# Retention followed by a leaky-ReLU MLP on one core: the order of ScalarE and VectorE work behind TensorE's products, and the engine that applies the masks

## The chip, the cores and the metric

One core of a Trainium2 chip. The metric is the device time of one execution in microseconds (us). Kernels sent together ran on the same chip, in alternation with the kernel before.

## The reference

Two stages. Retention: for 8 batches and 8 heads, scores of q and k are multiplied by a decay that depends on the distance and applied to v. Then an MLP over the 4608 resulting tokens.

```python
scores = scale * np.matmul(q, k.transpose(0, 1, 3, 2))       # q, k, v: (8, 8, 576, 64)
ret = scores * Dmat[None]                                    # gamma ** (i - j), i >= j
x = np.matmul(ret, v)                                        # -> 4608 tokens x 512
h = x @ w_in                                                 # 512 x 2048
g = np.maximum(0.01 * h, h)
return g @ w_out                                             # 2048 x 512
```

## The kernel before

Retention is done in 36 units of 128 tokens, as linear attention with a running state; four units make a set of 512 tokens for the MLP. From set 2 on, both layers save matmuls by Strassen-like schemes: seven products in place of eight, with sums of operands made beforehand (`sum_x` on GpSimd, `mix` on VectorE) and sums of products made while the PSUM banks are read (`plus`, `keep`, `give`). While a set goes through the MLP, four "bursts" of the next units' retention are put between its products: two in the first layer (`at_step(5)`, `at_step(6)`), two in the second (`at_step(7)`, `at_step(8)`). The first layer's group of seven:

```python
    def h_seven(g, f, fill, middle=None):
        ...

        def plus(name, a, b):
            r[name] = m_pool.tile([P, 2, HT], FP, name=name)
            nc.vector.tensor_tensor(out=r[name], in0=r[a], in1=r[b], op=ADD)

        def give(i, k, name):
            leaky(g_tile(g)[:, f + i * HF : f + i * HF + 2, k * HT : (k + 1) * HT], r[name])

        product("p1", w_sub(f, 0, 0), x_sub(g, 0, 0), True)
        r["k1"] = m_pool.tile([P, 2, HT], FP, name="k1")
        nc.scalar.copy(out=r["k1"], in_=r["p1"])
        fill[0]()
        product("p1", w_sub(f, 0, 1), x_sub(g, 1, 0), False)
        give(0, 0, "p1")
        fill[1]()
        product("p6", w[:, 1], t[:, 1], True)
        plus("u2", "p6", "k1")
        product("p5", w[:, 0], t[:, 0], True)
        plus("v", "p5", "u2")
        if middle is not None:
            middle()
        fill[2]()
        product("p7", w[:, 2], t[:, 2], True)
        plus("h4", "p7", "v")
        product("p5", w[:, 3], x_sub(g, 1, 1), False)
        plus("h5", "p5", "u2")
        give(1, 1, "h4")
        fill[3]()
        give(0, 1, "h5")
        product("p7", w_sub(f, 1, 1), t[:, 3], False)
        plus("h4", "p7", "u2")
        give(1, 0, "h4")
```

`middle` is the burst. `fill` are ordinary blocks of the first layer that give the other engines time. p1, p5 and p7 are accumulated into twice; a second pass must wait until the first result has been read out of its bank: k1 is such a reading (by ScalarE), h4 and `v` are others (by VectorE).

The burst, the masks and the loop over the sets:

```python
    def masks(u, aside=False):
        s16s[u] = b_pool.tile([P, 2, NP, CH], F16, name="s16")
        if aside:
            nc.scalar.copy(out=s16s[u], in_=sc_tiles[u][:, :, 0])
            nc.gpsimd.tensor_tensor(
                out=s16s[u],
                in0=s16s[u],
                in1=mask16.unsqueeze(1).unsqueeze(1).to_broadcast([P, 2, NP, CH]),
                op=MUL,
            )
            return
        nc.vector.tensor_tensor(
            out=s16s[u],
            in0=sc_tiles[u][:, :, 0],
            in1=mask_sb.unsqueeze(1).unsqueeze(1).to_broadcast([P, 2, NP, CH]),
            op=MUL,
        )

    def burst(u, out=True):

        if u < NU:
            scores(u)
        if out:
            outputs(u - 1)
        if u < NU:
            masks(u, u > 12)
            state(u, 0)
            state(u, 1)
            state_cast(u, pool_copy)
        if out:
            own(u - 1)
            add(u - 1)
        ...

        def at_step(n):
            return (lambda: step(4 * g + n)) if more else None

        h_seven(g, 0, [block(2), block(10), block(3), block(11)], at_step(5))
        mix(g, 0, 0)
        mix(g, 1, 0)
        h_seven(g, 4, [block(6), block(7), block(14), first], at_step(6))
        mix(g, 2, 0)
        h_block(g, 15)
        for n in range(3):
            mix(g, n, 1)
        others({0: [at_step(7)], 4: [at_step(8)]} if more else {})
```

For units after the twelfth, ScalarE copies the scores out of PSUM and GpSimd, which gets its operands from SBUF here, multiplies by the mask. `state` adds to the running state on VectorE; at every fourth chunk it needs a further multiplication by the decay, with both operands in SBUF (line 275; it is called the "scaled addition" below, though it is a multiplication).

## Time and profile before

| | before |
|---|---|
| time, median of 3 runs first, of 6 with those beside the change | 294.28, 294.17 us |
| profiled span | 292.0 us |
| TensorE / VectorE / ScalarE / GpSimd busy | 276.3 / 211.7 / 158.3 / 160.7 us |
| length of a set (sets 2 to 7, from one first copy of p1 to the next) | 29.5 to 30.6 us |
| holes over 0.1 us in TensorE's stream in sets 2 to 8, by cause: K, H, M, X | 6.25, 2.26, 1.36, 0.43 us |

A hole is read from the starts of two matmuls; the wait that the timeline prints in brackets is smaller, as it counts from the modelled end of the last matmul. K is the wait for the copy k1, H the one for the addition h4, M the one for the mixing addition, X the one for GpSimd's input sums.

### The profile page before, as it was taken

Reading aid. Unit: us, or ns where it says so; the run is one execution under the profiler, and the core shown is the slowest. Engines: PE = TensorE matmul, PEld = TensorE weight load, DVE = VectorE, ACT = ScalarE, POOL = GpSimd, SP = SyncE. Lnnn points to the kernel's source line nnn. Section 1 sums busy time; section 2 is a strip of 40 time slices with the busy share of each in tenths; the row PEclk is TensorE's granted clock in tenths of the full one; section 3 lists DMA queues with packets and bytes.
Section 4 is the critical chain, followed back from the end, with each engine's and each line's share of the span. In section 5 each row is a group of like instructions: output and inputs, shape, how many; then the busy total and the mean of one; then the engine's idle time right before and its main releaser. Section 6 shows DMA issues by size and latency. Waiting matters only on the chain.

```text
span 292.0 us, 9901 instructions
## 1 busy us (share of the span) xinstructions
PE 276.3 (95%) x4279; PEld 205.0 (70%) x4279; DVE 211.7 (73%) x352; ACT 158.3 (54%) x292; POOL 160.7 (55%) x175
## 2 busy tenths in 40 slices
PE   7799999999999999899979998999899998999994
PEld 2478889547876787578747875687578856785774
DVE  2983787987857795779586968886779577866572
ACT  4676767425247824782477357644765376517520
POOL 8968503563385649554964489438943892151000
PEclk9999999999999999999999999999999999999999
DMA  8999999999999979973999589668976341011003
GB/s 218 295 234 226 275 205 222 188 200 195 243 232 295 225 149 243 219 167 87 181 250 175 122 186 257 142 140 169 270 145 147 71 147 38 2 74 72 2 0 144
DMA packets 131739, 50.03 MB, mean 171 GB/s; under 512 B 121264, under 2 KB 126000, under 8 KB 131696
## 3 DMA queue, kind: packets, MB, share of 16 engines
q1 hardware_dynamic: 125392, 39.59, 60.2%
q0 software_dynamic: 6016, 9.70, 14.9%
q8 instruction: 33, 0.54, 0.8%
q10 hardware_dynamic: 288, 0.11, 0.2%
q14 instruction: 10, 0.08, 0.1%
HBM read 36.81 MB, written 9.44 MB: 158 GB/s over the span
## 4 chain that ended last, share of the span: by engine, by line
PE 69%; DVE 16%; ACT 8%; DMA 2%; issue 2%; POOL 2%; DVEq 0%; ACTq 0%; POOLq 0%
PE acc L588 27%; PE acc L390 19%; PE acc L470 12%; ACT gt L404 6%; PE acc L525 5%; DVE mix L569 5%; DVE h L481 3%; PE sc L220 2%; DMA t<-in_q_dram 2%; DVE s L271 1%; DVE xT L377 1%; DVE s L275 1%; ACT k L488 1%; DVE v L481 1%; PE sc L229 1%
## 5 line engine op out<-in xcount | busy, mean ns | idle before, releaser
L390 PE MATMUL acc<-xT,w_in 128*128 128x512 f16 (+2 forms) x544 | 88.7, 304 | 0.3 <-DVE xT L377 0.2
L404 ACT ACTIVATE gt<-acc 128x512 f16<-128x512 f32 x102 | 60.0, 597 | 17.9 <-PE acc L390 16.3
L588 PEld LDWEIGHTS <-gt 128*128 128x128 f16 x640 | 61.2, 98 | 8.5 <-ACT gt L404 0.8
L390 PEld LDWEIGHTS <-w_in 128*128 128x128 f16 x544 | 46.3, 98 | 17.4 <-issue 0.3
L240 POOL TENSOR_TENSOR s<-s,idle 128x512 f16<-128x512 f16 x23 | 27.3, 1186 | 41.9 <-ACT s L239 41.9
L588 PE MATMUL acc<-w_out,gt 128*128 128x256 f16 x384 | 46.3, 273 | 0.2 <-ACT gt L404 0.2
L177 POOL TENSOR_TENSOR qk<-t,cs 128x512 f16<-128x512 f32 x28 | 30.3, 1082 | 19.8 <-DMA t<-in_q_dram 19.8
L239 ACT CAST s<-sc 128x512 f16<-128x512 f32 x23 | 13.4, 584 | 36.1 <-PE sc L229 36.1
L404 ACT ACTIVATE gt<-h 128x512 f16<-128x512 f32 x42 | 25.9, 628 | 12.4 <-DVE h L481 11.8
L181 POOL TENSOR_TENSOR v<-t,cs 128x512 f16<-128x512 f32 x28 | 30.1, 1076 | 1.7 <-DMA t<-in_v_dram 1.4
L588 PE MATMUL acc<-w_mix,mix 128*128 128x256 f16 x256 | 30.3, 273 | 0.4
L588 PE MATMUL acc<-w_mix,gt 128*128 128x256 f16 x256 | 30.6, 273 | 0.0
L481 DVE TENSOR_TENSOR u<-acc,k 128x512 f32<-128x512 f32 x14 | 9.7, 691 | 26.6 <-PE acc L470 26.6
L470 PEld LDWEIGHTS <-w_sum 128*128 128x128 f16 x224 | 21.9, 98 | 9.1 <-issue 0.5
L174 ACT CAST qk<-t 128x512 f16<-128x512 f32 x36 | 22.6, 627 | 10.5 <-DMA t<-in_k_dram 10.5
L588 PEld LDWEIGHTS <-mix 128*128 128x128 f16 x256 | 24.5, 98 | 4.9 <-DVE mix L569 2.0
L470 PEld LDWEIGHTS <-w_in 128*128 128x128 f16 x168 | 15.9, 97 | 15.6 <-issue 7.1
L372 ACT COPY own<-ot 128x512 f32<-128x512 f32 x33 | 19.5, 591 | 12.6 <-PE ot L316 7.1
L287 POOL CAST st<-s 128x512 f16<-128x512 f32 x21 | 13.0, 621 | 23.9 <-DVE s L275 10.2
L377 DVE TENSOR_TENSOR xT<-ot,own 128x512 f16<-128x512 f32 x33 | 22.5, 682 | 4.9 <-ACT own L372 4.9
L481 DVE TENSOR_TENSOR h<-acc,u 128x512 f32<-128x512 f32 x28 | 19.2, 685 | 8.4 <-PE acc L470 8.4
L470 PE MATMUL acc<-x_sum,w_sum 128*128 128x256 f16 x168 | 22.9, 272 | 0.3 <-POOL x_sum L457 0.3
(77 smaller groups left out, 424.8 us busy)
## 6 DMA issues: line engine op xcount, KB each, us to landing
out_dram<-osb SPq DMA_DIRECT2D x17, 512.0 KB, 4.3
t<-in_k_dram SPq DMA_DIRECT2D x27, 256.0 KB, 3.6
t<-in_q_dram SPq DMA_DIRECT2D x26, 256.0 KB, 4.0
t<-in_v_dram SPq DMA_DIRECT2D x25, 256.0 KB, 4.5
w_in<-in_moe_w_in_dram POOLq DMA_DIRECT2D x8, 256.0 KB, 6.7
w_out<-in_moe_w_out_dram POOLq DMA_DIRECT2D x4, 512.0 KB, 10.0
t<-in_v_dram POOLq DMA_DIRECT2D x7, 256.0 KB, 5.3
t<-in_q_dram POOLq DMA_DIRECT2D x6, 256.0 KB, 5.6
```

The lines of the kernel that those rows point to most:

```text
L174: nc.scalar.copy(out=qk16[u][:, 1], in_=t32[u, 1])
L177: eng.tensor_tensor(out=qk16[u][:, 0], in0=t32[u, 0], in1=decay(u, 0), op=MUL)
L181: eng.tensor_tensor(out=v16[u], in0=t32[u, 2], in1=decay(u, 1), op=MUL)
L240: nc.gpsimd.tensor_tensor(out=s16s[u], in0=s16s[u], in1=mask16.unsqueeze(1).unsqueeze(1).to_broadcast([P, 2, NP, CH]), op=MUL,)
L372: nc.scalar.copy(out=owns[u], in_=ot_tiles[u][:, :, 0:NP].rearrange("q j c t -> q c j t"))
L377: nc.vector.tensor_tensor(out=x_of(u).rearrange("q (c g) t -> q c g t", g=2), in0=ot_tiles[u][:, :, NP : 2 * NP].rearrange("q g (c j) t -> ...
L390: nc.tensor.matmul(out=hps[:, n, :], lhsT=w_in16[:, c, f * P : (f + 1) * P], rhs=xT[g][:, c, ts], start=(c == 0), stop=(c == NP - 1),)
L404: nc.scalar.activation(out=out, in_=in_, func=mybir.ActivationFunctionType.Lrelu)
L470: nc.tensor.matmul(out=r[name][:, n, :], lhsT=lhs[:, c, n * P : (n + 1) * P], rhs=rhs[:, c, :], start=fresh and n == 0 and c == 0, stop=c ...
L481: nc.vector.tensor_tensor(out=r[name], in0=r[a], in1=r[b], op=ADD)
L525: nc.tensor.matmul(out=ys[tb], lhsT=g_t[0][:, f, tb * P : (tb + 1) * P], rhs=w_out16[:, f, :], start=(f == 0), stop=(f == NF - 1),)
L588: nc.tensor.matmul(out=r[name][tb][:, 0, :] if apart else r[name][0][:, tb, :], lhsT=lhs[:, f, tb * P : (tb + 1) * P], rhs=rhs[:, f, :], s ...
```

## The change

The intent: (1) the last two activations of one group of seven go behind the next group's copy k1, so that this copy isn't held up, and the first two mixing additions (`mix`) go with them; (2) in the first layer's bursts, the output sum of the retention goes behind the two additions h4 and h5, which free banks of PSUM; (3) the masks of the two bursts in the second layer go from ScalarE and GpSimd to VectorE.

```diff
--- before.py
+++ after.py
@@ -456,7 +456,7 @@
         ):
             nc.gpsimd.tensor_tensor(out=t[:, n], in0=a, in1=b, op=SUB)
 
-    def h_seven(g, f, fill, middle=None):
+    def h_seven(g, f, fill, middle=None, owed=()):
 
         r = {}
         t = x_sums[g]
@@ -486,6 +486,8 @@
         product("p1", w_sub(f, 0, 0), x_sub(g, 0, 0), True)
         r["k1"] = m_pool.tile([P, 2, HT], FP, name="k1")
         nc.scalar.copy(out=r["k1"], in_=r["p1"])
+        for late in owed:
+            late()
         fill[0]()
         product("p1", w_sub(f, 0, 1), x_sub(g, 1, 0), False)
         give(0, 0, "p1")
@@ -494,19 +496,19 @@
         plus("u2", "p6", "k1")
         product("p5", w[:, 0], t[:, 0], True)
         plus("v", "p5", "u2")
-        if middle is not None:
-            middle()
+        settled = middle() if middle is not None else None
         fill[2]()
         product("p7", w[:, 2], t[:, 2], True)
         plus("h4", "p7", "v")
         product("p5", w[:, 3], x_sub(g, 1, 1), False)
         plus("h5", "p5", "u2")
+        if settled is not None:
+            settled()
         give(1, 1, "h4")
         fill[3]()
-        give(0, 1, "h5")
         product("p7", w_sub(f, 1, 1), t[:, 3], False)
         plus("h4", "p7", "u2")
-        give(1, 0, "h4")
+        return [lambda: give(0, 1, "h5"), lambda: give(1, 0, "h4")]
 
 
 
@@ -780,19 +782,21 @@
             mix(g, n, 0)
             mix(g, n, 1)
 
-    def burst(u, out=True):
+    def burst(u, out=True, split=False):
 
         if u < NU:
             scores(u)
         if out:
             outputs(u - 1)
         if u < NU:
-            masks(u, u > 12)
+            masks(u, split)
             state(u, 0)
             state(u, 1)
             state_cast(u, pool_copy)
         if out:
             own(u - 1)
+            if split:
+                return lambda: add(u - 1)
             add(u - 1)
 
     def ahead(u, between=None):
@@ -810,10 +814,11 @@
         if u < NU:
             load(u)
 
-    def step(u):
-        burst(u)
+    def step(u, split=False):
+        rest = burst(u, True, split)
         fetch(u + 4)
         ahead(u + 2, (lambda: sum_x(u // 4 - 1)) if u % 4 == 0 else None)
+        return rest
 
 
     halves(0, (0, 1))
@@ -934,13 +939,17 @@
         def block(f):
             return lambda: h_block(g, f)
 
-        def at_step(n):
-            return (lambda: step(4 * g + n)) if more else None
-
-        h_seven(g, 0, [block(2), block(10), block(3), block(11)], at_step(5))
-        mix(g, 0, 0)
-        mix(g, 1, 0)
-        h_seven(g, 4, [block(6), block(7), block(14), first], at_step(6))
+        def at_step(n, split=False):
+            return (lambda: step(4 * g + n, split)) if more else None
+
+        owed = h_seven(
+            g, 0, [block(2), block(10), block(3), block(11)], at_step(5, True)
+        )
+        owed += [lambda: mix(g, 0, 0), lambda: mix(g, 1, 0)]
+        for late in h_seven(
+            g, 4, [block(6), block(7), block(14), first], at_step(6, True), owed
+        ):
+            late()
         mix(g, 2, 0)
         h_block(g, 15)
         for n in range(3):
```

## The prediction

> **What bounds the kernel now.** I read the page first (shares, clock, chain), then the waits of one set, then the timeline of that set. A "set" is 512 tokens; sets 2 to 8 run the loop that the change edits, sets 0 and 1 and the start do not. The page says that TensorE is the bound, at full clock:
>
> ```profile
> span 292.0 us, 9901 instructions
> ...
> PE 276.3 (95%) x4279; PEld 205.0 (70%) x4279; DVE 211.7 (73%) x352; ACT 158.3 (54%) x292; POOL 160.7 (55%) x175
> ...
> PEclk9999999999999999999999999999999999999999
> ...
> PE 69%; DVE 16%; ACT 8%; DMA 2%; issue 2%; POOL 2%; DVEq 0%; ACTq 0%; POOLq 0%
> ```
>
> No other engine is near full, so only holes in TensorE's stream can be won. A quarter of the chain runs over VectorE and ScalarE: places where TensorE waits for a particular result. The stretch in steady state from 202.4 to 232.3 us (set 6) has these TensorE waits:
>
> ```profile
> PE acc L470 <- ACT k L488: 0.7, 1, 0.7
> ...
> PEld L470 <- DVE h L481: 0.7, 1, 0.7
> PEld L588 <- DVE mix L569: 0.3, 1, 0.3
> ```
>
> Modelled ends hide part of a hole, so I size holes from starts: start of a matmul less start of the one before, less its pitch in an unbroken run (216 ns for 512 columns, 108 ns for 256; four blocks of 4x512 start 0.86 us after one another). The timeline of set 6 shows the three holes and what makes them:
>
> ```profile
> 207.75 0.68 DVE L377 TENSOR_TENSOR xT<-ot,own 128x512 f16<-128x512 f32 x1
> ...
> 208.34 0.68 DVE L481 TENSOR_TENSOR h<-acc,v 128x512 f32<-128x512 f32 x1
> ...
> 209.08 0.61 PE L470 MATMUL acc<-x_sum,w_in 128*128 128x256 f16 x4 [0.19 <-DVE h L481]
> 209.53 0.60 PE L470 MATMUL acc<-xT,w_in 128*128 128x256 f16 x4
> ...
> 210.07 1.14 ACT L404 ACTIVATE gt<-h 128x512 f16<-128x512 f32 x2
> ...
> 211.11 0.57 ACT L488 COPY k<-acc 128x512 f32<-128x512 f32 x1
> ...
> 211.74 0.60 PE L470 MATMUL acc<-xT,w_in 128*128 128x256 f16 x4 [0.75 <-ACT k L488]
> ...
> 221.24 1.19 POOL L240 TENSOR_TENSOR s<-s,idle 128x512 f16<-128x512 f16 x1 [1.90 <-ACT s L239]
> 221.45 1.53 DVE L569 TENSOR_TENSOR mix<-mix,gt 128x1024 f16<-128x1024 f16 x1
> ...
> 223.03 2.52 PEld L588 LDWEIGHTS <-mix 128*128 128x128 f16 x24 [0.34 <-DVE mix L569]
> ```
>
> - **Hole K (0.91 us).** The second group of seven starts with product p1 at 209.53; its partial sum is in PSUM by 210.13. The copy k1 of it could run at about 210.16, but ScalarE first does the two last activations of the first group (210.07, x2; the second waits for VectorE's last addition) and copies at 211.11. The next matmul onto that bank comes at 211.74 instead of 210.83.
> - **Hole H (0.35 us).** p7 is accumulated into a second time, so TensorE waits until VectorE has read it (h4, 208.34); the output sum xT sits in front of h4, at 207.75.
> - **Hole M (0.23 us).** The mixed operand of the second layer is late because one VectorE addition took 1.53 us, not its usual 0.69, beside the GpSimd mask at 221.24. The same addition took 1.52 or 1.53 us in each of sets 2 to 7, and 0.69 in set 8, which has no mask.
>
> Over the sets 2, 3, 4, 5, 6, 7, 8 the holes are: K 0.85, 0.91, 0.91, 0.91, 0.91, 0.91, 0.85 (sum 6.25); H 0, 0.14, 1.18, 0, 0.35, 0.59, 0 (sum 2.26); M 0.23, 0.22, 0.23, 0.23, 0.23, 0.22, 0 (sum 1.36). Together 9.87 us.
>
> **What the Trainium skill says.** (1) "TensorE: Matmul & The Clock Gate", Architectural detail: ScalarE and VectorE queues are "strict FIFO". The trace agrees: k1's input was ready 0.95 us before the copy, which kept its place in the queue. So the order in the program is what counts, and that is what is changed. (2) "SBUF — State Buffer", Who interferes with whom: a VectorE instruction with two SBUF inputs contends with a GpSimd instruction that reads SBUF, and the later one is blocked. The 1.53 against 0.69 us agrees; a mask out of PSUM has one SBUF input and should stay out of this. (3) "PSUM — Partial Sum Buffer", PSUM bank collisions: two engines must not touch one bank at once, even to read, and the compiler puts a dependency between them. The trace has VectorE's state addition waiting 0.3 to 0.4 us for ScalarE's copy of the mask's input out of the same score tile, so a mask on VectorE costs the states less than its own length.
>
> **Part 1, last activations behind the next copy.** Nothing is added or removed; two activations move behind k1, and two mixing additions move into the next group, where on VectorE they still stand before its first addition u2. In set 6: with part 2, p7's second pass starts at 208.73, p1 at 209.16, its sum is readable 0.63 later, at 209.79. ScalarE by then has done the first activation and that of block 11 (start 208.97, pitch 0.5), so k1 starts at 209.79 and TensorE may go on 0.63 later (as 211.11 to 211.74), at 210.42. Block 6 keeps it busy from 209.59 to 210.46. Hole K closes, with 0.04 us to spare. The deferred work: ScalarE at 210.27 and 210.77 the two activations, at 211.27 block 6, done 211.9; its bank is the one that p5 takes at 212.18, 0.3 us later. VectorE: mixing from 210.92 to about 212.7, then u2 (ready at 212.4), v done at 214.0; p5 is accumulated into at 214.65. Nothing blocks TensorE here, but margins are some tenths. Gain: up to 6.25; for margins this thin I take off 0.5.
>
> **Part 2, output sums behind the bank-freeing additions.** The xT sum (pitch 0.60 on VectorE) moves behind h4 and h5, so h4 comes 0.6 us sooner where the states and not the product are last. Hole H falls by min(hole, 0.6): 0.14 + 0.58 to 0.60 + 0.35 + 0.59 = 1.68 us; set 4, whose state update with a decay takes 1.08 us beside GpSimd, keeps about 0.6. The sum is needed only for the next set, and its bank pair only one burst later, over 5 us away.
>
> **Part 3, masks.** It removes 11 ScalarE copies (0.58 each) and 11 GpSimd multiplications (1.19), and adds 11 VectorE multiplications out of PSUM (about 0.69, pitch 0.60); counted by comparing the instruction order of both kernels, for two bursts per set, one in the last with bursts. None of the removed time is on the path itself. What it buys is the 0.83 us that hole M's addition loses: M closes, 1.36 us. What it costs: in the first burst the mask stands after the mixing, so minus 0.83 plus 0.60 leaves the later additions no later than now. In the last burst the states start about 0.12 us later, and through GpSimd's cast and input sums (x_sum) so does the next set. There set 5 already waits 0.43 us for x_sum and set 6 has no slack. Cost about 0.2 us.
>
> **Sum.** 6.25 - 0.5 + 1.68 + 1.36 - 0.2 = 8.6 us. 294.28 - 8.6 = 285.7, so I say 285.8 us, a gain of 2.9%.
>
> **Rivals.**
> (a) *The wait moves.* With a gain of 1.3 us a set, the deferred activations and mixing hold up the second group instead: through the bank of p5 (0.3 us to spare), through v (0.6), or through x_sum. For it: three thin margins, and mixing took from 0.69 to 1.48 us in different sets depending on GpSimd. Against: each margin above was positive by the measured pitches. If half of K came back, 3.1 us would go: about 289, near the 2% line.
> (b) *VectorE becomes the bound or delays the second layer.* It is at 73%; with 11 x 0.69 = 7.6 us more, less 6 x 0.83 = 5.0, it is near 75% of a shorter span. Against it: in the stretch of the second layer it still waits about 1 us for products before its output additions. If masks delayed every set by 0.4 us, it would be 288.
> (c) *Loads or transposes become the bound.* The DMA share in sets 2 and 3 is 0.94 and 0.81, and 4% more speed asks 4% more. Against: no TensorE wait there names a DMA, and loads are issued some two bursts before their use; the later sets have 0.2 to 0.75. If set 2 gave its gain back: about 287.
> (d) *Only the masks or only the sums matter*, with K caused by the chain through VectorE's last addition. Against: k1 depends only on p1's sum, and after the change no VectorE result stands before it but h4. It would leave 291.
>
> **Range and chances.** 2% is 5.9 us, that is 288.4. All holes gone and no new wait would be 284.2; I put the low end at 284.6. The high end, 288.8, is a combination of (a) and (c). Faster by over 2%: 0.85; within 2%: 0.14 (rival a in full, or d); slower: 0.01, as the same matmuls are issued and no bank is held longer.
>
> **What would show it.** Right, if on the profile after: the wait of the matmul for k1 (0.7 a set) is gone or under 0.15; the wait for h is left only in set 4, at about half; the second mixing addition takes 0.69 in all sets and the weight load's wait for it is gone; ScalarE and GpSimd busy time fall by about 6 and 13 us and VectorE rises by 2 to 3; a set takes 28.3 to 28.6 us instead of 29.6 to 30.3. Wrong, if TensorE now waits for an activation (bank of p5), for v, or longer for x_sum, by over 0.3 us a set; or if the clock falls below 1.00.

## The result

284.33 us (median of 6 runs, 283.96 to 285.82) against 294.17 us: the ratio is 0.966, 95% interval 0.963 to 0.969. A ratio here is the mean time of one kernel's fast runs over that of the other's fast runs of the same rounds, so it is not quite the ratio of the medians. The gain is 9.8 us where 8.5 were foretold, and the time lies 0.3 us below the stated range: the prediction was wrong on the size, in the direction of caution.

The page of the changed kernel, its shares, clock and chain:

```profile
span 282.4 us, 9912 instructions
...
PE 273.2 (97%) x4279; PEld 205.7 (73%) x4279; DVE 210.1 (74%) x363; ACT 152.6 (54%) x281; POOL 148.3 (53%) x164
...
PEclk9999999999999999999999999999999999999999
...
PE 87%; POOL 4%; DVE 3%; DMA 2%; issue 1%; ACT 0%; POOLq 0%; DVEq 0%
```

TensorE has the same 4279 matmuls at the same clock in 9.6 us less. VectorE and ScalarE have left the chain: 16% and 8% before, 3% and 0% now. The timeline of set 6 after the change (start, duration, engine, line, operation):

```profile
202.08 0.69 DVE L481 TENSOR_TENSOR h<-acc,v 128x512 f32<-128x512 f32 x1
...
202.68 0.68 DVE L481 TENSOR_TENSOR h<-acc,u 128x512 f32<-128x512 f32 x1
...
203.17 0.60 PE L470 MATMUL acc<-x_sum,w_in 128*128 128x256 f16 x4
...
203.28 0.68 DVE L377 TENSOR_TENSOR xT<-ot,own 128x512 f16<-128x512 f32 x1
...
204.30 0.59 ACT L488 COPY k<-acc 128x512 f32<-128x512 f32 x1 [0.33 <-PE acc L470]
...
204.78 1.15 ACT L404 ACTIVATE gt<-h 128x512 f16<-128x512 f32 x2
...
204.94 0.60 PE L470 MATMUL acc<-xT,w_in 128*128 128x256 f16 x4
...
214.65 0.69 DVE L571 TENSOR_TENSOR mix<-mix,gt 128x1024 f16<-128x1024 f16 x1
```

The sum xT now stands behind both additions, and p7's second pass (203.17) has no wait. The copy k1 waits for TensorE (the bracket at 204.30), and TensorE hardly waits for it any more: p1 goes on 0.64 us later, 0.03 us after the block before it would have let it. The two activations follow at 204.78. The mixing addition takes 0.69 us, not 1.53.

Holes over 0.1 us of the changed kernel in sets 2 to 8: none of K, H and M; X 0.25 us, in set 6. Smaller ones are left or new: K 0.03 us in each of the seven sets (0.20 in all), X 0.03 us in set 2 and 0.07 to 0.08 us in sets 3 to 5 (0.25 in all). Before, the only small ones of these two kinds and of H were X 0.03 us in set 2 and H 0.06 us in set 5. With these counted, K fell from 6.25 to 0.20 us, H from 2.33 to 0, M from 1.36 to 0, and X rose from 0.46 to 0.50: 9.7 us of holes are gone. Sets take 28.0 to 28.5 us. From set 2's first copy to the end the execution is 10.1 us shorter (198.9 against 209.0 us); what the four kinds do not cover is spread over gaps that I have not traced. The span fell by 9.6 us, as set 2 began 0.4 us later in this execution (83.44 against 83.02 us); this start lies before everything the change touches and varied from 82.7 to 83.4 us over all runs here.

### The profile page after: what moved, and what is told of

Read it like the earlier page. It is cut to its first block, busy times and chain, and to the rows that moved or that the text cites. A ratio compares the mean times of both kernels' runs of the same rounds, so it can differ in the third digit from the quotient of the medians.

```text
span 282.4 us, 9912 instructions
## 1 busy us (share of the span) xinstructions
PE 273.2 (97%) x4279; PEld 205.7 (73%) x4279; DVE 210.1 (74%) x363; ACT 152.6 (54%) x281; POOL 148.3 (53%) x164
## 4 chain that ended last, share of the span: by engine, by line
PE 87%; POOL 4%; DVE 3%; DMA 2%; issue 1%; ACT 0%; POOLq 0%; DVEq 0%
PE acc L590 33%; PE acc L390 26%; PE acc L470 15%; PE acc L527 5%; POOL t L134 3%; PE sc L220 3%; DMA w_in<-in_moe_w_in_dram 2%; PE ot L305 2%; PE ot L316 2%; PE sc L229 1%; POOL x_sum L457 1%; DVE s L247 1%; PE acc L202 0%; DVE stmp L274 0%; DVE xT L377 0%
## 5 line engine op out<-in xcount | busy, mean ns | idle before, releaser
L404 ACT ACTIVATE gt<-acc 128x512 f16<-128x512 f32 x102 | 58.3, 597 | 14.5 <-PE acc L390 14.3
L590 PE MATMUL acc<-w_mix,mix 128*128 128x256 f16 x256 | 29.3, 273 | 0.0
L240 POOL TENSOR_TENSOR s<-s,idle 128x512 f16<-128x512 f16 x12 | 14.5, 1207 | 15.9 <-ACT s L239 15.9
L571 DVE TENSOR_TENSOR mix<-gt 128x1024 f16<-128x1024 f16 x16 | 13.7, 861 | 9.5 <-ACT gt L404 9.5
```

Source lines behind the costliest of these rows:

```text
L240: nc.gpsimd.tensor_tensor(out=s16s[u], in0=s16s[u], in1=mask16.unsqueeze(1).unsqueeze(1).to_broadcast([P, 2, NP, CH]), op=MUL,)
L404: nc.scalar.activation(out=out, in_=in_, func=mybir.ActivationFunctionType.Lrelu)
L590: nc.tensor.matmul(out=r[name][tb][:, 0, :] if apart else r[name][0][:, tb, :], lhsT=lhs[:, f, tb * P : (tb + 1) * P], rhs=rhs[:, f, :], s ...
```

## The experiments

The theory after the result: the three parts do what they were meant to, and two more waits went that I had booked as staying or growing, both because GpSimd's multiplications had lengthened a VectorE addition with two operands in SBUF. The rivals: that the parts' gains overlap or that part of the gain is chance; that set 4's wait for h was closed by the reordering alone; that the margins around k1 matter less than I thought.

All kernels gave correct results. Holes over 0.1 us are summed over sets 2 to 8 of each profiled execution. The change ran earlier than e1 to e8, with its own runs of the kernel before (294.17 us); run again later, as e10, it took 284.08 us, ratio 0.963 (0.960 to 0.966).

| kernel | us, median | ratio to before (95%) | span | K | H | M | X |
|---|---|---|---|---|---|---|---|
| before (beside the eight below) | 294.06 | 1 | 292.0 | 6.25 | 2.26 | 1.36 | 0.43 |
| the change | 284.33 | 0.966 (0.963 to 0.969) | 282.4 | 0 | 0 | 0 | 0.25 |
| e1: activations alone | 288.24 | 0.980 (0.978 to 0.982) | 285.5 | 0 | 1.92 | 1.35 | 0.44 |
| e2: sums alone | 292.69 | 0.995 (0.994 to 0.997) | 290.5 | 6.71 | 0.59 | 1.36 | 0.44 |
| e3: masks alone | 291.94 | 0.993 (0.991 to 0.995) | 290.1 | 6.24 | 1.54 | 0 | 0.43 |
| e4: the change without masks | 286.10 | 0.974 (0.972 to 0.975) | 284.1 | 0 | 0.59 | 1.36 | 0.44 |
| e5: masks of the first burst only | 285.33 | 0.971 (0.969 to 0.973) | 282.9 | 0 | 0.59 | 0 | 0.43 |
| e6: masks of the last burst only | 285.52 | 0.971 (0.970 to 0.973) | 283.9 | 0 | 0 | 1.35 | 0.14 |
| e7: e4, product behind cast | 285.48 | 0.971 (0.969 to 0.972) | 283.6 | 0 | 0 | 1.43 | 0.43 |
| e8: the change, one activation deferred | 285.25 | 0.971 (0.969 to 0.972) | 283.5 | 1.39 | 0 | 0 | 0.43 |

Span less these four sums is 281.4 to 282.4 us for every row, so the four kinds of hole account for the differences between the kernels to within 1 us; less the time at which set 2 starts, the rows lie within 0.7 us.

**e1, part 1 alone.** The changed kernel with `add` back in the burst and masks by the old rule.

```diff
-            if split:
-                return lambda: add(u - 1)
-            masks(u, split)
+            masks(u, u > 12)
```

> Part 1 alone (activations behind the next copy; sums and masks as before). Theory: the waits for k1 (K) go in all seven sets, 6.25 us, and nothing else changes: the additions h (H, 2.26 us), the mixing addition (M, 1.36) and the input sums of set 5 (0.43) keep their holes. Time about 288.0 us. Rival (margins of some tenths give part of K back through the bank of p5 or v): 289 to 291, with a wait of the p5 product for an activation of 0.2 us or more a set.

Measured 288.24 us. K is gone but for 0.03 us a set and nothing is given back: no wait of over 0.1 us for p5's bank or for v appears. H is 0.34 us smaller as well, in set 6, which the expectation did not foresee. Part 1 is worth 6.05 of the 6.25 us.

**e2, part 2 alone.** The activations and the two mixing additions back in their places, masks by the old rule.

```diff
+        give(0, 1, "h5")
         product("p7", w_sub(f, 1, 1), t[:, 3], False)
         plus("h4", "p7", "u2")
-        return [lambda: give(0, 1, "h5"), lambda: give(1, 0, "h4")]
+        give(1, 0, "h4")
+        return []
...
-            masks(u, split)
+            masks(u, u > 12)
...
-        owed += [lambda: mix(g, 0, 0), lambda: mix(g, 1, 0)]
...
+        mix(g, 0, 0)
+        mix(g, 1, 0)
```

> Part 2 alone (output sums behind the bank-freeing additions). Theory: H shrinks by 1.68 us to about 0.6, all of it left in set 4, but K is not moved by it and may grow by up to 0.3 us in some sets, since the second deferred activation still waits for VectorE's last addition, which now stands behind the sum. Time 292.6 to 293.4 us. Rival (H closes in set 4 by the reordering itself): no wait for h left in set 4, 292.0 us.

292.69 us. H falls to 0.59 us, all in set 4, as I had predicted for part 2. K grows by 0.46 us, so alone this part earns less than with part 1: there the activation that waits for VectorE's last addition no longer stands before k1.

**e3, part 3 alone.** Activations, mixing additions and sums as before; the edits that put the activations and the mixing back are those of e2 and are left out here.

```diff
-            if split:
-                return lambda: add(u - 1)
```

> Part 3 alone (masks of the second-layer bursts on VectorE). Theory (GpSimd's multiplications lengthen VectorE additions with two SBUF operands): M goes (1.36 us), the scaled state addition at the last burst of set 4 takes 0.42 us, not 0.95, so that set 5's wait for its input sums (0.43) goes as well; K is untouched. In set 4 the scaled state addition of the first half may or may not meet the mask of its own burst: H there 1.18 or 0.6. Time 291.8 to 292.6 us. Rival (only M): 292.8 us with the 0.43 us wait still there. Rival (a mask delays VectorE): 293 us or more.

291.94 us. M is gone. X moved from set 5 to set 6 (0.43 us in each case). H changed too, from 0.14, 1.18, 0.35 and 0.59 us in sets 3, 4, 6 and 7 to 0.49, 0.52, 0 and 0.53: moving masks shifts GpSimd against VectorE in every set, and what it lengthens differs from set to set. In set 3 the scaled addition took 0.85 us in place of 0.43, and H there rose by 0.35 us.

**e4, the change without part 3.**

```diff
-            masks(u, split)
+            masks(u, u > 12)
```

> The changed kernel without part 3 (parts 1 and 2). Theory: K gone, H gone but for about 0.6 us in set 4 (its scaled state addition takes 1.08 us beside GpSimd's multiplication), M there in six sets (1.36), set 5's wait for input sums there (0.4 or more). Time 284.3 + 1.36 + 0.6 + 0.2 to 0.4 = 286.5 to 286.8 us. Rival (H in set 4 was closed by part 2 itself): no wait for h in set 4 and 285.9 us.

286.10 us, below the 286.5 expected: set 2 began 0.3 us sooner (83.14 against 83.44), and X costs no more than in the changed kernel, whose holes under 0.1 us make up for its smaller sum. H in set 4 is 0.59 us and X 0.44: both are back without the masks, so the reordering did not close them.

**What lengthens the scaled addition.** The timelines of set 4, TensorE's matmul behind h4 with them. Before:

```profile
146.75 1.16 POOL L240 TENSOR_TENSOR s<-s,idle 128x512 f16<-128x512 f16 x1
147.10 1.08 DVE L275 TENSOR_TENSOR s<-stmp,cs 128x256 f32<-128x256 f32 x1
...
149.44 0.61 PE L470 MATMUL acc<-x_sum,w_in 128*128 128x256 f16 x4 [1.02 <-DVE h L481]
```

The changed kernel without masks (e4):

```profile
144.83 1.16 POOL L240 TENSOR_TENSOR s<-s,idle 128x512 f16<-128x512 f16 x1
145.19 1.08 DVE L275 TENSOR_TENSOR s<-stmp,cs 128x256 f32<-128x256 f32 x1
146.93 0.61 PE L470 MATMUL acc<-x_sum,w_in 128*128 128x256 f16 x4 [0.42 <-DVE h L481]
```

The changed kernel:

```profile
145.16 0.42 DVE L275 TENSOR_TENSOR s<-stmp,cs 128x256 f32<-128x256 f32 x1
145.23 1.37 POOL L240 TENSOR_TENSOR s<-s,idle 128x512 f16<-128x512 f16 x1
146.31 0.60 PE L470 MATMUL acc<-x_sum,w_in 128*128 128x256 f16 x4
```

Where GpSimd's product starts first, the addition takes 1.08 us; where the addition is first, if only by 0.07 us, it takes 0.42 us and the product takes 1.37 us in place of 1.16. Counted from the first copy of p1 in the set, the product started at 4.65 us before and at 5.15 us in the changed kernel, the addition at 5.00 and 5.08 us. GpSimd's half microsecond comes from its cast of the states, earlier in its queue. By the trace of the changed kernel this cast waits 1.54 us for VectorE's state addition, which has a mask in front of it, and starts 2.00 us before the set's first copy of p1; before, and in e5 below, it starts 2.50 us before it. From there to the product GpSimd works with hardly a break in all three. That the overlap is the cause, and that the masks of the last burst are, e5 and e7 test.

**e5, masks of the first second-layer burst only on VectorE.**

```diff
-            masks(u, split)
+            masks(u, u > 12 and u % 4 != 3)
```

> The changed kernel with the masks of the last burst of each set back on ScalarE and GpSimd; wait: of the two second-layer bursts this variant gives the one whose unit number leaves 3 when divided by 4 (the first of the two) VectorE, the other the old way. Theory: M stays closed (mixing addition 0.69 us in all sets), and what part 3 did unforeseen comes back: the scaled state addition at the last burst of set 4 takes 0.95 us again, set 5 waits 0.4 us or more for its input sums, and set 4's wait for h is back with about 0.6 us. Time 284.3 + 1.0 = 285.3 us. Rival (these two were closed by parts 1 and 2): 284.3 us.

285.33 us; M closed, the wait for h in set 4 (0.59) and X in set 5 (0.43) back. The masks of the last burst are what closes these two.

**e6, masks of the last burst only on VectorE.**

```diff
-            masks(u, split)
+            masks(u, u > 12 and u % 4 != 0)
```

> The changed kernel with the masks of the first second-layer burst back on ScalarE and GpSimd and those of the last one on VectorE. Theory: M is back in six sets, 0.23 us each (mixing addition 1.5 us), the rest as in the changed kernel: no wait for h in set 4, no or little wait for input sums in set 5. Time 284.3 + 1.36 = 285.7 us. Rival (M was never on the path): 284.3 us.

285.52 us; M is back in six sets with 0.22 to 0.23 us each, set 4's wait for h stays closed, and set 5's for the input sums is 0.08 us; set 3 waits 0.14 us for its input sums. The two halves of part 3 work apart from each other.

**e7, e4 with GpSimd's product behind its cast of the states** in the first layer's bursts. ScalarE's copy keeps its place; no mask moves to another engine.

```diff
-            masks(u, split)
+            masks(u, u > 12, split)
             state(u, 0)
             state(u, 1)
             state_cast(u, pool_copy)
+            if split:
+                masks(u, False, True)
```

The first call now makes ScalarE's copy alone in these bursts and the second one GpSimd's product (the edit of `masks` itself is left out).

> As the changed kernel without part 3, but in the two bursts of the first layer GpSimd's multiplication stands behind GpSimd's cast of the states, so it cannot run during the state additions (the cast waits for them). Theory (contention between that multiplication and the scaled state addition keeps the wait for h in set 4): scaled additions there take 0.42 us, H in set 4 is gone though no mask has moved to VectorE; set 5's wait for input sums and M stay, so 0.6 us under the changed kernel without part 3. Rival (the wait in set 4 has another cause, such as where GpSimd stands): no gain.

285.48 us, 0.62 us under e4. Set 4 of this kernel:

```profile
145.19 0.43 DVE L279 TENSOR_TENSOR s<-stmp,cs 128x256 f32<-128x256 f32 x1
...
145.68 0.61 POOL L291 CAST st<-s 128x512 f16<-128x512 f32 x1 [0.80 <-DVE s L279]
146.25 1.16 POOL L244 TENSOR_TENSOR s<-s,idle 128x512 f16<-128x512 f16 x1
...
146.34 0.60 PE L474 MATMUL acc<-x_sum,w_in 128*128 128x256 f16 x4
```

The addition starts at 145.19 as in e4, takes 0.43 us and not 1.08, and TensorE's wait for h is gone. With the same work on the same engines and only the overlap taken away, this shows that the overlap made the wait.

**e8, only the last activation deferred.**

```diff
+        give(0, 1, "h5")
         product("p7", w_sub(f, 1, 1), t[:, 3], False)
         plus("h4", "p7", "u2")
-        return [lambda: give(0, 1, "h5"), lambda: give(1, 0, "h4")]
+        return [lambda: give(1, 0, "h4")]
```

> The changed kernel with only the last activation (the one that waits for VectorE's last addition) behind k1, and the one before it in front of k1 as before. ScalarE started k1 0.93 us after its last start in four sets and 0.69 to 0.72 in three, and one activation takes 0.5 us of its order: k1 is late by 0.07 us in four sets and 0.3 us in three. Theory: holes at k1 of about 0.1 and 0.3 us, 1.2 us in all: 285.5 us. Rival (ScalarE's whole length counts): 0.5 us a set, 3.5 us, 287.8. Rival (only the wait for VectorE mattered): 284.3 us.

285.25 us. K is 0.30, 0.33 and 0.33 us in sets 3, 4 and 7 and 0.11 us in each of the other four, 1.39 us in all (1.2 expected). Set 4:

```profile
147.26 0.62 ACT L404 ACTIVATE gt<-h 128x512 f16<-128x512 f32 x1
...
147.78 0.58 ACT L488 COPY k<-acc 128x512 f32<-128x512 f32 x1
...
148.40 0.60 PE L470 MATMUL acc<-xT,w_in 128*128 128x256 f16 x4 [0.17 <-ACT k L488]
```

The hole of 0.11 us shows in starts alone, as no wait is printed in brackets. In set 2:

```profile
90.17 1.03 PE L390 MATMUL acc<-xT,w_in 128*128 128x512 f16 x4
...
90.51 0.58 ACT L488 COPY k<-acc 128x512 f32<-128x512 f32 x1
...
91.14 0.60 PE L470 MATMUL acc<-xT,w_in 128*128 128x256 f16 x4
```

The block's four matmuls take 0.86 us, but p1 goes on 0.97 us after the block's start, and 0.63 us after k1's. So most of K (4.9 of 6.25 us) came from the last activation, the one that waits for VectorE, and one 0.5 us activation more in front of k1 costs only what it overruns.

**e9 and e11, the holes that are left.** Two further edits. In e11 GpSimd makes the input sums ahead of the cast of q; e9 has this, and in the last set only product p7 runs one half of the tokens after the other. e10 is the changed kernel again.

```diff
         if u < NU:
             cast_k(u)
-            cast_q(u, nc.gpsimd)
         if between is not None:
             between()
         if u < NU:
+            cast_q(u, nc.gpsimd)
             cast_v(u, nc.gpsimd)
```

> The changed kernel with the input sums before the cast of q, nothing else: 0.25 us under the changed kernel if the wait of set 6 was all there was to win; equal if it comes back as a wait for transposes.

> The changed kernel with two more edits for the holes that it leaves: GpSimd makes the input sums of the next set before the cast of q (one cast, 1.0 us, sooner), and in the last set only product p7 runs one half of the tokens after the other, so the last p1 product reads the latest activations half a product later. Expected: the wait of set 6 for input sums (0.25 us) gone, the two waits for activations in the last set (0.38 and 0.15 us) gone or under 0.1 us: 0.25 + 0.45 = 0.7 us under the changed kernel of the same call. Rival (the cast of q, 4.5 us later, makes transposes late for the second burst of the next set): a wait of a burst's weight load for a transfer, and no gain or a loss.

> The changed kernel itself, again, for comparison on the same chip: 284.0 to 284.6 us; the waits for k1, h and the mixing addition at zero, one wait for input sums of 0.25 us or so.

e10 took 284.08 us, e11 289.74 us, e9 287.77 us (the kernel before 295.10 us beside them; one run of e11, 293.46 us, was slow and is in neither its median here nor its ratio of 0.981). The rival of e9's expectation came true, and the loss, 5.7 us in e11 and 3.7 in e9, is larger than either text allowed for. X is gone, but TensorE now waits for transposes, 5.17 us in e11 and 4.71 us in e9. In set 2 of e9 (SPq is the queue that issues transfers):

```profile
97.08 1.64 SPq L185 DMA_TRANSPOSE qkT<-qk  x1
...
100.81 0.32 PE L220 MATMUL sc<-qkT 64*64 64x64 f16 x16 [2.30 <-DMA qkT<-qk]
```

A transpose lands 3.7 us after its issue (median of this stretch); in the changed kernel the one for this burst was issued at 94.67 us, 4.5 us before the burst. The later casts of q pushed this slack under zero. Part of the loss may be the clock: in seven of these two kernels' ten fast executions the granted clock was 0.992 to 0.994, where it was 0.997 or more in every other fast execution. Why is not shown.

**e12, the last set's order alone.**

```diff
-                if last
+                if apart
                 else [(f, tb) for f in range(HF) for tb in range(2)]
```

> The changed kernel with the last set's order alone (only product p7 one half of the tokens after the other). The previous call's version with both edits had the tail after the last set's first copy at 28.63 us, against 29.08. Expected: the same 0.45 us here without the late transposes, so about 283.6 us, and the profile's tail at 28.6; the waits for activations in the last set gone.

283.59 us (283.44 to 284.22), ratio 0.964 (0.963 to 0.966). The product p1 of the last set, in the changed kernel and then in e12:

```profile
268.30 1.64 PE L590 MATMUL acc<-w_out,gt 128*128 128x256 f16 x12 [0.22 <-ACT gt L404]
```

```profile
267.36 1.91 PE L590 MATMUL acc<-w_out,gt 128*128 128x256 f16 x16
```

In the first the product breaks after four matmuls to wait for an activation; in the second its sixteen run without a break. Of the 0.53 us of such waits that went, 0.11 us came back as a wait for the mixing addition. From the last set's first copy to the end it is 28.64 us, against 29.07 and 29.08 in two executions of the changed kernel. By time alone the two kernels can't be told apart: the intervals of their ratios overlap. This is the fastest version tried.

## Why the prediction was wrong

What bounds the kernel and the three holes were right, and the changes of each hole were right in kind, but for H in set 4, which closed. The sum was mis-sized (holes under 0.1 us are counted here for K and X):

| term | predicted gain | measured in the holes |
|---|---|---|
| part 1 (K) | 6.25 - 0.5 = 5.75 | 6.05 |
| part 2 (H; in set 4 by part 3) | 1.68 | 2.26 |
| part 3, mixing (M) | 1.36 | 1.36 |
| part 3, later input sums (X) | -0.2 | -0.04 |
| sum | 8.6 | 9.6 |

- **"For margins this thin I take off 0.5."** The step worked out that p1's sum would be readable 0.63 us after p1's start, and k1 in time by 0.04 us. In the changed kernel k1 starts 0.69 us after p1's start, though it waits for p1 alone, and TensorE goes on 0.64 us after that; so k1 is late by 0.03 us in each of the seven sets. The margin was not there, yet missing it cost 0.20 us and not 0.5: each time only the overrun (in e8 0.11 us in four sets and 0.3 us in three).
- **"Set 4, whose state update with a decay takes 1.08 us beside GpSimd, keeps about 0.6."** This step failed. Part 2 alone does leave 0.59 us (e2, e4), but I took the 1.08 us over as fixed, having just named its cause for hole M: the overlap with a GpSimd product. I did not ask whether part 3, which moves GpSimd's work, would move this overlap as well. It did, by chance of order (0.07 us); e5 and e7 show it. In set 3 the same shift lengthened the scaled addition from 0.43 to 0.85 us. It cost nothing in the changed kernel, where part 2 brings h4 forward by 0.6 us; in e3, without part 2, H in set 3 rose by 0.35 us.
- **"Cost about 0.2 us" for the input sums.** The delay foretold is there: sets 3, 4 and 6 wait 0.07, 0.08 and 0.25 us that they did not wait before, 0.40 in all. What the step missed is the same error again: the scaled addition of set 4's last burst, on which set 5's input sums depend, took 0.95 us beside the mask that part 3 removes, and 0.42 us without it, and set 5's wait fell from 0.43 to 0.07 us (e6: 0.08 with the last burst's masks on VectorE; e5: 0.43 without).
- **The range.** The text itself gives 284.2 us for "all holes gone and no new wait" and then sets the low end at 284.6. The case that came was one I had written down and excluded. (The sum is a slip: 294.28 less the 9.87 us of holes is 284.4, still under the low end.) The three terms that were set too low, by 0.30, 0.58 and 0.16 us, make up the 1.0 us that was missed.

The rivals: the wait did not move to p5's bank, to v or, over 0.25 us, to the input sums (a); VectorE did not become the bound, and its busy time fell by 1.6 us where a rise of 2 to 3 was foretold, as additions got shorter beside GpSimd (b); no load or transpose came onto the path (c), though e9 and e11 show that transposes were nearer to it than I had thought: 0.7 us in one burst of set 2; and K went without the other parts (d, refuted by e1). ScalarE's and GpSimd's busy times fell by 5.7 and 12.4 us, as foretold.

## What to carry to other kernels

When one engine is the bound, list its holes by cause with sizes from start to start, and test each edit against each hole. Work in front of a result that the bound engine waits for can go behind it at no cost, as long as nobody waits for the moved work: here two activations behind a copy gave 6 of 10 us. And when an edit takes work off GpSimd or shifts it, treat every VectorE duration with two SBUF operands as open: 0.58 of the 1.0 us that I missed lay in one operation that I had taken over as a constant of 1.08 us.

## What the Trainium skill lacked or had wrong

- "SBUF — State Buffer", Who interferes with whom, says that issue order decides which engine is blocked, and, where it speaks of the two-port modes, that the later one is fully blocked. The runs agree on the order. In set 4 before, a full block until the product's end would have cost the addition 0.81 us; it lost 0.66. The sizes here: additions of 0.42 and 0.69 us became 0.95 to 1.08 and 1.53 us beside a GpSimd product of about 1.2 us, and a start 0.07 us sooner moved the loss to the product (1.37 us). What it lacks is the advice that a reorder can flip this in another place of the kernel than the one edited.
- "TensorE: Matmul & The Clock Gate", Back-to-back issue gap, gives about 131 ns a matmul for 512 columns in a stream with weight loads, and about 216 ns for an isolated one. Here four such matmuls in a stream, each with its weight load, started 0.86 to 0.87 us apart from the next group: 216 ns each. 131 ns was not seen.
- On no page did I find how to size a wait of TensorE in a profile. The wait printed for k1 was 0.75 us, by the modelled end of the matmul before; from start to start the hole was 0.91 us. Over the run the printed waits for k1 sum to 5.1 us and the holes to 6.25; the span of e1, which keeps 0.20 us of K, fell by 6.5 us, 0.34 of it from H.
